# Experts' blocks: rows turned in float32 by TensorE instead of by transposing DMA copies

## The chip, the cores and the metric

The kernel runs on one core of one Trainium2 chip. The metric is the device time in microseconds (us) of the whole program, one launch. The core has five engines that run side by side: PE (TensorE, matmuls and their weight loads), DVE (VectorE), ACT (ScalarE), POOL (GpSimd) and SP (SyncE, which here only issues transfers). Each works through its own instructions in order; semaphores make one wait for another.

## The reference

Three layers follow one another on 1792 tokens (4 batches of 448) with 768 columns:

```
scores = 30 * tanh(q k^T / 8 / 30);  attn = exp(scores - max) / sum;  x = attn v        # 4 batches, 12 heads of 64
logits = x @ w_gate + modality_bias[modality_id];  e = argmax(logits);  g = softmax(logits)[e]
x[mask_e] = g * (relu(x[mask_e] @ w1[e]) @ w2[e])                                        # 8 experts, 768 -> 1024 -> 768
out = (sigmoid(x @ w_gate2) * (x @ w_val)) @ w_out                                       # 768 -> 1536 -> 768
```

The experts' products are taken in float16 parts: each float32 operand is a first part (rounded to float16) and a second part (what is left, in float16). Three of the four products of parts are added up, so each float32 product costs three float16 ones.

## The kernel before

**Attention** (0 to 296 us of the trace) goes through 24 pairs of heads in 96 slots of key tiles (`qk`, `exps`, `av`). The work that follows a batch (sums, gate logits, routing, token rows) is put into slots of the next batch by the table `AFTER`. `end2` makes 128 columns of a batch's token rows: TensorE turns four tiles of `OT` (L441), DVE multiplies by the reciprocal sums into the float32 tile `x` (L446), DVE makes the first part (L457) and POOL the second (L461), both into `xr`, which `x_write` and, for the last batch, `x_put` store to the table `xs` in DRAM.

**Experts.** The tokens are sorted into blocks of 128 of one expert each; with these inputs there are 15 blocks, numbered s = 0 to 14. For a block, SP loads its token list (`load_idx`), POOL adds up its two parts and gathers the rows from `xs` into one of two buffers `xg` (`gather`), SP's transposing DMA turns the rows into `xT` (`trx`, L740), PE multiplies by `w1s` (`mm1`, 36 matmuls), ACT and DVE take relu and its two parts from PSUM (`relu`, L761 and L762), SP's transposing DMA turns them into `hT` (`trh`, L765), PE multiplies by `w2s` (`mm2`, 48 matmuls), ACT and DVE scale (`put_y`, L784 and L785) and POOL scatters the rows to `ys`.

`step(s)` writes this out by hand: first product of block s, second product of block s - 1, transposes for s and s + 2, gather for s + 4. Beside it, blocks 4 to 10 each carry a set of float64 weights of the last layer: two loads (L865), DVE's three bit operations on each (L878, L879, L880), an ACT scale, and a store (L904). From block 5 on SP also turns finished rows of `ys` by DMA (`y_load`, L971). Where a block's expert is new (here blocks 4 and 12), 3 MB of `w1` and 3 MB of `w2` are loaded and split by ACT and DVE (L714, L718) inside an `If`.

All instructions of an engine keep the written order (`tc.manual_schedule()`), and so do SP's transfers: one that waits holds up those behind it. `tr_tile` hands out the PSUM banks in `M["trs"]` in turn, four of them during the experts.

**Last layer** (641 us to the end): seven-product multiplications of quarters (L1042, L1022) with operands made by ACT, DVE and POOL.

Of the kernel before, what the change touches and what calls it, by code (L numbers as in the profile page):

```python
# [8 lines left out]
F32 = mybir.dt.float32  # L9
# [51 lines left out]
# slots, after the last one of a batch's pairs, of the work that follows it; the third batch's goes ahead of the experts  # L61
AFTER = ({'g0': 0, 'g1': 2, 's': 3, 'e1s': 4, 'e1g': 5, 'route': 6, 'route_b': 8, 'ga': 9, 'gb': 10, 'gc': 12, 'sc': (10, 12, 14, 16), 'e2': (7, 10, 12, 17, 21, 24), 'lo': (1, 1, 1, 1, 1, 1), 'xw': (26, 27)}, {'g0': 1, 'g1': 2, 's': 3, 'e1s': 4, 'e1g': 5, 'route': 6, 'route_b': 10, 'ga': 9, 'gb': 10, 'gc': 12, 'sc': (10, 12, 14, 16), 'e2': (7, 10, 12, 17, 20, 23), 'lo': (1, 1, 1, 1, 1, 0), 'xw': (26, 27)}, {'g0': 1, 'g1': 2, 's': 3, 'e1s': 5, 'e1g': 5, 'route': 6, 'route_b': 7, 'ga': 10, 'gb': 11, 'gc': 13, 'sc': (10, 11, 12, 13), 'e2': (6, 9, 10, 11, 12, 13), 'lo': (1, 1, 2, 1, 1, 1), 'xw': (15, 15), 'ta': (9, 9), 'w1': (11, 11, 14, 12, 13, 13), 'w1s': (14, 15, 17, 17, 18, 19), 'idx': 16, 'gather': (18, 19, 23), 'trx': (20, 22), 'w2': (20, 21, 22, 22)})
# [3 lines left out]
def tile_kernel(ctx: ExitStack, tc: tile.TileContext, q, k, v, cap, mod, wg, mb, w1, w2, gw, vw, ow, out, dbg=None):  # L66
# [305 lines left out]
    def end0g(b, pp):  # L372
        """the gate's products with the sums over the values"""
# [94 lines left out]
    def x_put(h):  # L468
        """half of the last batch's columns"""
        c = DM // 4  # L470
        for a in range(2):
            w = slice(2 * c * a + c * h, 2 * c * a + c * h + c + (XW - DM if a == h == 1 else 0))
            nc.sync.dma_start(out=xs[(B - 1) * S:N, w].rearrange("(p c) n -> p c n", c=4), in_=xr[B - 1][:, :, w])

# [19 lines left out]
    def route_b(b):  # L494
        """place of each token in its expert's list: tokens of the expert before it"""
# [263 lines left out]
    def relu():  # L759
        hi, lo = (M["h"][:, a].rearrange("p (n f) -> p n f", n=2) for a in range(2))  # L760
# [38 lines left out]
    def step(s, fill=((), ()), more=None):  # L799
        """first product of block s, second product of block s - 1"""  # L800
# [8 lines left out]
        trh(s)  # L809
# [14 lines left out]
        mm2(s - 1)  # L824
# [842 lines left out]
```

## Time and profile before

| | us |
|---|---|
| median of three runs | 1146.42 (1144.09 to 1157.45) |
| span of the profiled execution | 1146.1 |
| attention, to the first product of block 0 | about 296 |
| blocks, to the end of the last second product | about 345 |
| last layer | about 505 |

No time from outside is given for the profiled execution, so its span stands for its time. PE is busy 930.1 us (81%), DVE 757.9, POOL 534.2, ACT 466.5. The page's slices show the DMA engines nearly full from the 14th slice to the 22nd, most of the stage of the blocks, and far less after that. A line such as L777 in the page is a line of this kernel; a group's idle time names what ended it.

### The profile page before, as it was taken

The numbers are of one execution on the slowest core, as the hardware profiler recorded it, in microseconds if no ns is written. First come the engines' busy times: TensorE is split into PE (matmuls) and PEld (weight loads), VectorE is DVE, ScalarE is ACT, GpSimd is POOL, SyncE is SP. The second block draws the span as 40 slices with busy tenths as digits, with TensorE's granted clock in tenths as the row PEclk, the third lists the DMA queues.
The fourth block names the chain that finished last, engine by engine and source line by source line (L and its number), as shares of the span: only waits on it lengthen the run. The fifth ranks groups of instructions, "written<-read, shape, count | busy, mean of one in ns | idle before, by whom it ended". The sixth has DMA issues, their size and how long they took to land. (4 is left out here: it accounts for less than half of the span.)

```text
span 1146.1 us, 14196 instructions
## 1 busy us (share of the span) xinstructions
PE 930.1 (81%) x4752; PEld 449.5 (39%) x4752; DVE 757.9 (66%) x1059; ACT 466.5 (41%) x734; POOL 534.2 (47%) x515
## 2 busy tenths in 40 slices
PE   7878677776877867795956788778898889999996
PEld 2223222222343433352523433333355545666653
DVE  7899989899662443435542389988657874543661
ACT  6656555555311332102331255445334434554330
POOL 5545536545432312214233577876603437877031
PEclk9898888887998989799979898999999999999998
DMA  9888976877756999999888333322304213220001
GB/s 200 173 192 142 169 174 109 163 154 183 203 130 143 206 210 184 244 194 260 144 201 117 114 122 123 113 97 83 110 15 96 84 55 97 84 70 28 1 28 55
DMA packets 202123, 150.98 MB, mean 132 GB/s; under 512 B 142240, under 2 KB 183088, under 8 KB 202032
## 3 DMA queue, kind: packets, MB, share of 16 engines
q1 hardware_dynamic: 196864, 130.37, 52.2%
q0 software_dynamic: 5168, 19.54, 6.5%
q8 instruction: 40, 0.66, 0.2%
q14 instruction: 51, 0.42, 0.1%
HBM read 87.05 MB, written 26.94 MB: 99 GB/s over the span
## 5 line engine op out<-in xcount | busy, mean ns | idle before, releaser
L777 PE MATMUL sc<-w2s,hs 128*128 128x384 f16 x720 | 133.6, 351 | 68.7 <-DMA hs<-hs 32.7
L1042 PEld LDWEIGHTS <-wa 128*128 128x128 f16 x909 | 90.5, 100 | 114.7 <-issue 39.3
L756 PE MATMUL sc<-w1s,xT 128*128 128x512 f16 x540 | 124.1, 390 | 12.2 <-DMA xT<-xg 12.2
L1042 PE MATMUL pp<-yr,wa 128*128 128x512 f16 (+1 forms) x468 | 107.8, 385 | 28.9 <-DVE zr L1072 12.9
L777 PEld LDWEIGHTS <-hs 128*128 128x128 f16 x720 | 74.5, 104 | 128.3 <-issue 45.6
L325 ACT ACTIVATE E<-sc,sct 128x896 f32<-128x896 f32 x72 | 72.4, 1005 | 95.2 <-PE sc L316 94.7
L940 POOL TENSOR_TENSOR wa<-sta,wa 128x384 f16<-128x384 f32 x87 | 92.1, 1073 | 6.5 <-ACT wa L935 6.4
L913 DVE TENSOR_TENSOR sta<-sta 128x384 f32<-128x384 f32 x96 | 89.6, 971 | 2.1 <-POOL y L940 0.7
L316 PE MATMUL sc<-qT,kT 128*128 128x448 f16 x288 | 77.2, 396 | 13.7 <-DMA qT<-qT 10.1
L756 PEld LDWEIGHTS <-xT 128*128 128x128 f16 x540 | 53.6, 100 | 79.1 <-DMA xT<-xg 13.7
L350 POOL TENSOR_TENSOR w2s<-E 128x896 f32<-128x896 f32 x24 | 51.5, 2146 | 63.5 <-ACT E L330 63.3
L1042 PE MATMUL pp<-zr,wa 128*128 128x384 f16 x441 | 75.7, 326 | 0.6 <-ACT yr L1090 0.6
L1042 PE MATMUL pp<-wos,yr 128*128 128x384 f16 x378 | 67.3, 343 | 10.3 <-ACT hs L1135 10.3
L330 ACT ACTIVATE E<-E,capt 128x896 f32<-128x896 f32 x72 | 74.7, 1038 | 0.6
L339 PE MATMUL ot<-E,vf 128*64 128x448 f32 x288 | 72.5, 586 | 0.0
L725 POOL TENSOR_TENSOR idx<-idx 128x1 f32<-128x1 f32 x19 | 6.9, 363 | 119.5 <-DMA idx<-lists 119.3
L935 ACT ACTIVATE wa<-sta 128x384 f16<-128x384 f32 x98 | 48.5, 513 | 23.5 <-DVE sta L913 19.7
L352 POOL TENSOR_TENSOR w2s<-w2s,E 128x896 f32<-128x896 f32 x24 | 52.0, 2165 | 9.7 <-ACT E L330 8.6
L316 PEld LDWEIGHTS <-kT 128*128 128x128 f16 x288 | 25.3, 104 | 77.9 <-issue 48.9
L1042 PEld LDWEIGHTS <-wb 128*128 128x128 f16 x378 | 37.6, 100 | 44.3 <-issue 11.6
L1042 PEld LDWEIGHTS <-yr 128*128 128x128 f16 x378 | 38.6, 102 | 39.0 <-issue 16.6
L358 DVE TENSOR_TENSOR w2s<-w2s,EM 64x448 f32<-64x448 f32 x48 | 51.4, 1071 | 2.0 <-POOL w2s L352 1.5
(308 smaller groups left out, 1741.1 us busy)
## 6 DMA issues: line engine op xcount, KB each, us to landing
sta<-g SPq DMA_DIRECT2D x40, 384.0 KB, 3.0
st<-in_moe_w_dram SPq DMA_DIRECT2D x8, 1536.0 KB, 14.0
sta<-in_moe_w_val_dram SPq DMA_DIRECT2D x12, 768.0 KB, 7.9
sta<-in_moe_w_out_dram SPq DMA_DIRECT2D x12, 768.0 KB, 4.2
g<-sta SPq DMA_DIRECT2D x18, 384.0 KB, 5.8
qf<-in_q_dram SPq DMA_DIRECT2D x24, 224.0 KB, 4.0
qT<-qT SPq DMA_DIRECT2D x46, 112.0 KB, 3.1
kf<-in_k_dram SPq DMA_DIRECT2D x24, 192.0 KB, 3.3
```

What stands on the lines that cost most here:

```text
L316: nc.tensor.matmul(sc[:, h, :S], kt_[:, 3 * h + j], qt_[:, w, h], start=w == 0, stop=w == 1)
L325: nc.scalar.activation(out=e, in_=src, func=AF.Tanh, scale=sct)
L330: nc.scalar.activation(out=e, in_=e, func=AF.Exp, scale=capt)
L339: nc.tensor.matmul(ot[g][64 * h:64 * h + 64, :S], vf[g][:, h, j], e[:, h], start=j == 0, stop=False)
L350: nc.gpsimd.tensor_tensor(out=Tt[g], in0=Et[n - 1], in1=Et[n], op=ALU.add)
L352: nc.gpsimd.tensor_tensor(out=Tt[g], in0=Tt[g], in1=Et[n], op=ALU.add)
L358: nc.vector.tensor_tensor(out=Tt[g][p, h], in0=Tt[g][p, h], in1=e[p], op=ALU.add)
L756: nc.tensor.matmul(p[:, nh], xT[s % 2][:, a, kk], w1s[:, b_, kk, 512 * nh:512 * nh + 512], start=i == 0, stop=i == 17)
L777: nc.tensor.matmul(M["p2"][:, nh, :384], hT[par][:, a, kk], w2s[:, b_, kk, 384 * nh:384 * nh + 384], start=i == 0, stop=i == 23)
L913: tt = lambda eng, o, x, y, op: eng.tensor_tensor(out=o, in0=x, in1=y, op=op)
L940: los = [lambda x=x, d=d, e=e: e.tensor_tensor(out=d[1], in0=x, in1=d[0], op=ALU.subtract) for x, d, e in todo]
L1042: nc.tensor.matmul(bk[c][:, c0:c1], l(p, a, kk), r(p, b_, kk)[:, c0:c1], start=i == c0 == 0 and p in (1, 2, 7), stop=i == 3 * kn - 1 and c ...
```

## The change

`end2` writes float32 rows straight into `xr`; the split into two parts goes, with its temporary tiles and the entries `lo` of `AFTER`. So `xs` and the gathered rows hold float32 (the same bytes a row). A new helper `turned` lets PE turn float32 columns into two PSUM banks in turn; ACT copies each to the first parts, DVE takes the difference for the second parts. `trx` and `trh` call it in place of the transposing DMAs. `relu` becomes one ACT instruction that writes float32. In `step`, `trh(s)` stands between the two halves of `mm2(s - 1)`, and before the loop likewise. The other differences are removed comments and the views that go with these edits.

```
@@ end2
-        if spread:
-            xx = M["x32"][i]
-        else:
-            xx = tail.tile([112, 4, 2, D], F32, name="x32", tag="x32", bufs=2)
         nc.vector.tensor_tensor(
-            out=xx,
+            out=xr[b][:, :, 128 * i:128 * i + 128].rearrange("p c (a d) -> p c a d", a=2),
...
-        if spread:
-            nc.scalar.activation(out=hi, in_=src, func=AF.Copy)
-            end2_lo(b, i, nc.gpsimd if i in (0, 1, 3, 4, 5) else nc.vector)
-        else:
-            nc.vector.tensor_copy(hi, src)
-
-    def end2_lo(b, i, eng=nc.gpsimd):
-        src, hi, lo = x32.pop((b, i))
-        eng.tensor_tensor(out=lo, in0=src, in1=hi, op=ALU.subtract)
@@ x_put: two transfers of 1.5 KB a row in place of four of half that
+        w = slice(DM // 2 * h, (DM // 2, XW)[h])
+        nc.sync.dma_start(out=xs[(B - 1) * S:N, w].rearrange("(p c) n -> p c n", c=4), in_=xr[B - 1][:, :, w])
@@ transposes
+    def turned(dst, src, n):
+        for q_ in range(2):
+            pt = tr_tile()
+            for c in range(n):
+                w = 128 * (n * q_ + c)
+                nc.tensor.transpose(pt[:, 128 * c:128 * c + 128], src[:, w:w + 128], id32)
+            hi, lo = (dst[:, a, n * q_:n * q_ + n].rearrange("p k n -> p (k n)") for a in range(2))
+            nc.scalar.activation(out=hi, in_=pt[:, :128 * n], func=AF.Copy)
+            nc.vector.tensor_tensor(out=lo, in0=pt[:, :128 * n], in1=hi, op=ALU.subtract)
     def trx(s):
         nc.gpsimd.tensor_copy(gt[s % 4], xg[s % 2][:, DM:DM + 1])
-        nc.sync.dma_start_transpose(out=xT[s % 2].rearrange("p a k n -> p (a k) n"), in_=xg[s % 2].bitcast(F16)[:, 0:2 * DM])
+        turned(xT[s % 2], xg[s % 2], 3)
@@ relu, trh
-        nc.scalar.activation(out=hi, in_=M["p1"], func=AF.Relu)
-        nc.vector.scalar_tensor_tensor(out=lo, in0=M["p1"], scalar=0.0, in1=hi, op0=ALU.max, op1=ALU.subtract)
+        nc.scalar.activation(out=M["h"].rearrange("p (n f) -> p n f", n=2), in_=M["p1"], func=AF.Relu)
     def trh(s):
-        nc.sync.dma_start_transpose(out=hT[s % 2].rearrange("p a k n -> p (a k) n"), in_=M["h"].rearrange("p a f -> p (a f)"))
+        turned(hT[s % 2], M["h"], 4)
@@ step (and the same before the loop)
-        trh(s)
...
-        mm2(s - 1)
+        mm2(s - 1, (0,))
+        trh(s)
+        mm2(s - 1, (1,))
```

Where instructions stand now, at the two places on which the prediction turns. First PE just ahead of `mm1(2)`: the end of `mm2(0)` (input `hs`, weights `w2s`), then what follows. Before:

```order
L777 LDWEIGHTS hs
L777 MATMUL sc<-w2s,hs 128x384
L756 LDWEIGHTS xT_116
L756 MATMUL sc<-w1s,xT_116 128x512
L756 LDWEIGHTS xT_116
```

Now:

```order
L766 LDWEIGHTS hs
L766 MATMUL sc<-w2s,hs 128x384
L1349 UNCONDITIONAL_BRANCH
L1354 UNCONDITIONAL_BRANCH
L832 UNCONDITIONAL_BRANCH
L724 MATMUL tr<-id_85,xg_115 128x128 x6
L747 LDWEIGHTS xT_116
L747 MATMUL sc<-w1s,xT_116 128x512
```

The six transposes of `trx(3)` stand ahead of `mm1(2)`; before, they were a transfer on SP and PE went straight on.

Second DVE in `step(4)`, the first that carries float64 weights (`sta`): before, from the second part of relu to `put_y`:

```order
L762 SCALAR_TENSOR_TENSOR hs<-sc,hs 128x1024
L686 TENSOR_LOAD tib
L833 COMPARE_AND_BRANCH
L718 SCALAR_TENSOR_TENSOR w1s<-st_111,w1s 128x1024 x6
L833 UNCONDITIONAL_BRANCH x2
L878 TENSOR_SCALAR sta<-sta 128x768
L879 SCALAR_TENSOR_TENSOR sta<-sta 128x768
L880 SCALAR_TENSOR_TENSOR sta<-sta 128x768
```

Now:

```order
L727 TENSOR_TENSOR xT_116<-tr,xT_116 128x384 x2
L868 TENSOR_SCALAR sta<-sta 128x768
L869 SCALAR_TENSOR_TENSOR sta<-sta 128x768
L870 SCALAR_TENSOR_TENSOR sta<-sta 128x768
L868 TENSOR_SCALAR sta<-sta 128x768
L869 SCALAR_TENSOR_TENSOR sta<-sta 128x768
L870 SCALAR_TENSOR_TENSOR sta<-sta 128x768
L727 TENSOR_TENSOR hs<-tr,hs 128x512 x2
L774 SCALAR_TENSOR_TENSOR y<-sc,gt_131,y 128x768
```

The second parts of h (`hs<-tr`, the operand of `mm2(4)`) stood ahead of the float64 operations and stand behind them now.

## Rows read from the trace of the kernel before

**Rows 1.** Windows by stage: PE, PEld, DVE, ACT, POOL busy, PEclk, DMA, GB/s.

```profile
0.00:296.00 296.00, 219.10 (x1005) 75.82 (x1005) 268.50 (x395) 169.25 (x199) 159.85 (x130) 0.88 0.79 165
...
390.00:641.00 251.00, 190.25 (x974) 98.49 (x972) 105.82 (x131) 59.58 (x75) 73.14 (x102) 0.89 0.99 195
641.00:935.00 294.00, 248.85 (x1193) 120.21 (x1192) 236.04 (x277) 130.50 (x257) 167.15 (x138) 0.94 0.29 90
```

**Rows 2.** Timeline of PE, blocks 3 to 14: start, us, work, idle before.

```profile
382.82 9.41 PE L756 MATMUL sc<-w1s,xT 128*128 128x512 f16 x36 [4.70 <-DMA xT<-xg]
...
399.87 7.93 PE L756 MATMUL sc<-w1s,xT 128*128 128x512 f16 x36
419.06 10.07 PE L777 MATMUL sc<-w2s,hs 128*128 128x384 f16 x48 [11.26 <-DMA hs<-hs]
...
591.96 10.65 PE L777 MATMUL sc<-w2s,hs 128*128 128x384 f16 x48 [13.14 <-DMA hs<-hs]
...
611.88 7.96 PE L777 MATMUL sc<-w2s,hs 128*128 128x384 f16 x48 [1.49 <-ACTq L802]
621.92 3.11 PE L1042 MATMUL pp<-yr,wa 128*128 128x256 f16 x27 [2.08 <-DMA perm<-idx,dix]
631.79 9.52 PE L777 MATMUL sc<-w2s,hs 128*128 128x384 f16 x48 [6.76 <-ACTq L1447]
```

**Rows 3.** Timeline of SP (transfers issued), blocks 4 to 14 and their ends.

```profile
394.57 17.26 SPq L765 DMA_TRANSPOSE hs<-hs  x1
...
413.03 5.20 SPq L740 DMA_TRANSPOSE xT<-xg  x1
...
614.67 2.04 SPq L765 DMA_TRANSPOSE hs<-hs  x1
618.53 1.69 SPq L740 DMA_TRANSPOSE xT<-xg  x1
```

**Rows 4.** DMA issues of the whole program: count, us from issue to landing.

```profile
yr<-ys SPq DMA_TRANSPOSE x8, 5.9
```

**Rows 5.** Timeline of PE around block 2.

```profile
319.69 1.47 PE L441 MATMUL tr<-id,OT 128*112 128x128 f32 x12
321.00 7.96 PE L777 MATMUL sc<-w2s,hs 128*128 128x384 f16 x48
328.80 7.93 PE L756 MATMUL sc<-w1s,xT 128*128 128x512 f16 x36
```

**Rows 6.** Timeline of SP in the same stretch.

```profile
333.54 3.46 SPq L473 DMA_DIRECT2D xs<-xr  x4
337.09 5.58 SPq L765 DMA_TRANSPOSE hs<-hs  x1
343.55 3.97 SPq L722 DMA_DIRECT2D idx<-lists  x4
351.58 1.53 SPq L740 DMA_TRANSPOSE xT<-xg  x1
```

**Rows 7.** Timeline of POOL and DVE in the same stretch.

```profile
347.70 1.00 POOL L734 DMA_INDIRECT xg<-xs,idx  x1 [0.67 <-POOL idx L727]
...
360.54 1.01 POOL L734 DMA_INDIRECT xg<-xs,idx  x1 [0.28 <-POOL idx L727]
...
333.58 0.09 DVE L546 MEMSET xr<- 112x32 f32 x1 [3.98 <-POOL xr L461]
```

**Rows 8.** Groups by line: count, busy us, mean ns of one, idle before.

```profile
L457 DVE CAST xr<-x 112x512 f16<-112x512 f32 x18 | 14.1, 783 | 0.6
...
L1072 DVE TENSOR_TENSOR hs<-hs,pp 128x512 f32<-128x512 f32 x18 | 12.2, 679 | 5.2 <-PE pp L1042 3.8 <-ACT sta L935 1.4
L1090 ACT ACTIVATE hs<-pp 128x512 f32<-128x512 f32 x18 | 10.4, 580 | 4.3 <-PE pp L1042 4.3
```

**Rows 9.** Groups by line, DVE alone, from 345 to 641 us.

```profile
L879 DVE SCALAR_TENSOR_TENSOR sta<-sta 128x768 int32<-128x768 int32 x14 | 13.4, 960 | 0.5
...
L878 DVE TENSOR_SCALAR sta<-sta 128x768 int32<-128x768 int32 x14 | 7.8, 559 | 51.8 <-DMA sta<-in_moe_w_val_dram 32.6 <-DMA sta<-in_moe_w_gate_dram 19.0
```

More of the change, by code (lines that the diff above doesn't have):

```diff
@@ L60 @@
 ZBT = (0, 0, 0, 1, 1, 2, 3, 5, 6)
-AFTER = ({'g0': 0, 'g1': 2, 's': 3, 'e1s': 4, 'e1g': 5, 'route': 6, 'route_b': 8, 'ga': 9, 'gb': 10, 'gc': 12, 'sc': (10, 12, 14, 16), 'e2': (7, 10, 12, 17, 21, 24), 'lo': (1, 1, 1, 1, 1, 1), 'xw': (26, 27)}, {'g0': 1, 'g1': 2, 's': 3, 'e1s': 4, 'e1g': 5, 'route': 6, 'route_b': 10, 'ga': 9, 'gb': 10, 'gc': 12, 'sc': (10, 12, 14, 16), 'e2': (7, 10, 12, 17, 20, 23), 'lo': (1, 1, 1, 1, 1, 0), 'xw': (26, 27)}, {'g0': 1, 'g1': 2, 's': 3, 'e1s': 5, 'e1g': 5, 'route': 6, 'route_b': 7, 'ga': 10, 'gb': 11, 'gc': 13, 'sc': (10, 11, 12, 13), 'e2': (6, 9, 10, 11, 12, 13), 'lo': (1, 1, 2, 1, 1, 1), 'xw': (15, 15), 'ta': (9, 9), 'w1': (11, 11, 14, 12, 13, 13), 'w1s': (14, 15, 17, 17, 18, 19), 'idx': 16, 'gather': (18, 19, 23), 'trx': (20, 22), 'w2': (20, 21, 22, 22)})
+AFTER = ({'g0': 0, 'g1': 2, 's': 3, 'e1s': 4, 'e1g': 5, 'route': 6, 'route_b': 8, 'ga': 9, 'gb': 10, 'gc': 12, 'sc': (10, 12, 14, 16), 'e2': (7, 10, 12, 17, 21, 24), 'xw': (26, 27)}, {'g0': 1, 'g1': 2, 's': 3, 'e1s': 4, 'e1g': 5, 'route': 6, 'route_b': 10, 'ga': 9, 'gb': 10, 'gc': 12, 'sc': (10, 12, 14, 16), 'e2': (7, 10, 12, 17, 20, 23), 'xw': (26, 27)}, {'g0': 1, 'g1': 2, 's': 3, 'e1s': 5, 'e1g': 5, 'route': 6, 'route_b': 7, 'ga': 10, 'gb': 11, 'gc': 13, 'sc': (10, 11, 12, 13), 'e2': (6, 9, 10, 11, 12, 13), 'xw': (15, 15), 'ta': (9, 9), 'w1': (11, 11, 14, 12, 13, 13), 'w1s': (14, 15, 17, 17, 18, 19), 'idx': 16, 'gather': (18, 19, 23), 'trx': (20, 22), 'w2': (20, 21, 22, 22)})
 @with_exitstack
@@ L433, in rows, with end2 @@
         return xr[b]
-    x32 = {}
-    def end2(b, i, spread=False):
+    def end2(b, i):
         rows(b)
@@ L441, in end2 @@
             nc.tensor.transpose(xp[:112, 128 * c:128 * c + 128], OT[NPAIR * b + i][:, 112 * c:112 * c + 112], id32)
-        if spread:
-            xx = M["x32"][i]
-        else:
-            xx = tail.tile([112, 4, 2, D], F32, name="x32", tag="x32", bufs=2)
         nc.vector.tensor_tensor(
-            out=xx,
+            out=xr[b][:, :, 128 * i:128 * i + 128].rearrange("p c (a d) -> p c a d", a=2),
             in0=xp[:112].rearrange("p (c a d) -> p c a d", c=4, a=2),
             in1=recs[b][:, :, 2 * i:2 * i + 2].rearrange("p c (a o) -> p c a o", o=1).to_broadcast([112, 4, 2, D]), op=ALU.mult)
-        hi, lo = (xr[b].bitcast(F16)[:, :, DM * a + 128 * i:DM * a + 128 * i + 128] for a in range(2))
-        src = xx.rearrange("p c a d -> p c (a d)")
-        x32[b, i] = src, hi, lo
-        if spread:
-            nc.scalar.activation(out=hi, in_=src, func=AF.Copy)
-            end2_lo(b, i, nc.gpsimd if i in (0, 1, 3, 4, 5) else nc.vector)
-        else:
-            nc.vector.tensor_copy(hi, src)
-    def end2_lo(b, i, eng=nc.gpsimd):
-        src, hi, lo = x32.pop((b, i))
-        eng.tensor_tensor(out=lo, in0=src, in1=hi, op=ALU.subtract)
     def x_write(b, h):
@@ L468, in x_put @@
     def x_put(h):
[L470 to L473, printed above, removed]
+        w = slice(DM // 2 * h, (DM // 2, XW)[h])
+        nc.sync.dma_start(out=xs[(B - 1) * S:N, w].rearrange("(p c) n -> p c n", c=4), in_=xr[B - 1][:, :, w])
     def route(b):
@@ L759, in relu @@
     def relu():
-        hi, lo = (M["h"][:, a].rearrange("p (n f) -> p n f", n=2) for a in range(2))
-        nc.scalar.activation(out=hi, in_=M["p1"], func=AF.Relu)
-        nc.vector.scalar_tensor_tensor(out=lo, in0=M["p1"], scalar=0.0, in1=hi, op0=ALU.max, op1=ALU.subtract)
+        nc.scalar.activation(out=M["h"].rearrange("p (n f) -> p n f", n=2), in_=M["p1"], func=AF.Relu)
     def trh(s):
-        nc.sync.dma_start_transpose(out=hT[s % 2].rearrange("p a k n -> p (a k) n"), in_=M["h"].rearrange("p a f -> p (a f)"))
+        turned(hT[s % 2], M["h"], 4)
     def mm2(s, halves=(0, 1)):
@@ L1226, in tile_kernel @@
                 add(n0 + o["e2"][i], end2, b, i)
-                add(n0 + o["e2"][i] + o["lo"][i], end2_lo, b, i)
             for i in range(2):
@@ L1319, in tile_kernel @@
         hs = mid.tile([128, 6 * F], F16, name="hs")
-        M["h"] = hs[:, 0:2 * F].rearrange("p (a f) -> p a f", a=2)
+        M["h"] = hs[:, 0:2 * F].bitcast(F32)
         hT = [hs[:, 2 * F * i:2 * F * (i + 1)].rearrange("p (a k n) -> p a k n", a=2, k=8) for i in (1, 2)]
@@ L1324, in tile_kernel @@
         M["glast"] = mid.tile([128, 1], F32, name="glast")
-        M["x32"] = [yr[:112, 1024 * i:1024 * i + 1024].bitcast(F32).rearrange("p (c a d) -> p c a d", c=4, a=2) for i in range(12, 18)]
         st0 = yr[:, 0:12 * F].bitcast(F32).rearrange("p (k f) -> p k f", f=F)
@@ L1343, in tile_kernel @@
             scatter(B - 1, c)
-        end2(B - 1, 0, True)
-        end2(B - 1, 1, True)
+        end2(B - 1, 0)
+        end2(B - 1, 1)
         for c in range(2, 4):
             scatter(B - 1, c)
-        end2(B - 1, 2, True)
+        end2(B - 1, 2)
         split_w(st1, w2s, hi=None, parts=(5,))
         mm1(1, (1,))
-        end2(B - 1, 3, True)
-        end2(B - 1, 4, True)
-        end2(B - 1, 5, True)
+        end2(B - 1, 3)
+        end2(B - 1, 4)
+        end2(B - 1, 5)
         relu()
@@ L1359, in tile_kernel @@
         x_put(1)
-        trh(1)
         load_idx(3)
@@ L1363, in tile_kernel @@
             load_w(1, 1, st1, v2)
-        mm2(0)
+        mm2(0, (0,))
+        trh(1)
+        mm2(0, (1,))
         with if_new(1, [ENG.Activation, ENG.DVE]):
```

## The prediction

> **What bounds the kernel now.** I read the windows by stage first. In attention DVE is busy 268.5 of 296 us, in the stage of the blocks no engine is: PE has 190.25 of 251 us, DVE 105.82, but the DMA share is 0.99 at 195 GB/s [rows 1]. After 641 us the same engines move 90 GB/s at a share of 0.29, which is 90 / 0.29 = 310 GB/s when full [rows 1]. So the bytes of the blocks cost more DMA time than bytes elsewhere. Then PE's timeline: a block needs 7.93 us for its first product and 7.96 us for its second where PE was not waiting before [rows 2, 5], 15.9 us together, but from the start of `mm1(4)` at 382.82 to the end of `mm2(13)` at 611.88 + 7.96 = 619.84 us eleven steps take 237.0 us, 21.5 each [rows 2]. PE waits, and the longest waits are for transposes of h by DMA: 11.26 and 13.14 us, and the product that follows is itself longer, 10.07 and 10.65 us [rows 2]; I call such a first product after a wait cold. Last SP: a transpose held SP's queue for 17.26 us, others for 5.20 and 5.58 [rows 3, 6], and loads of lists and weights stand behind it. The blocks are bounded by the DMA engines and by SP's order, not by PE.
>
> **DMA time removed.** From 390 to 641 us eleven transposes of h go out (first at 394.57, last at 614.67) and eleven of x (first at 413.03, last at 618.53) [rows 3]. They carry 11 x (0.52 + 0.39) = 10.1 MB of 251 us x 195 GB/s = 48.9 MB; the eight `y_load` transposes [rows 4], which stay, carry 3.1. The other 35.7 MB at 310 GB/s take 115 us, so the transposes take 0.99 x 251 - 115 = 133 us. In tiles of 128 x 128 that is 11 x 28 + 8 x 12 = 404, so 0.33 us a tile (an estimate) and 9.2 us of all DMA engines a block. What stays is 251 - 101 = 150 us, under 14 us a block: DMA stops being the limit.
>
> The Trainium skill speaks against this: "Advanced Engine Details and Errata", section X-Bar Transpose (TRN2), says that transpose DMAs are as fast as regular ones. By that rule only 10.1 of 48.9 MB goes, 52 us of 251, and the DMA would still want 17.1 us a block; the rows above disagree with it, since the same engines reach 310 GB/s at full share elsewhere. It is the first rival below.
>
> **PE work added.** Fourteen float32 transposes a block, six for x and eight for h. Twelve of `OT` take 1.47 us end to end, the next matmul starting at 321.00, 1.31 after [rows 5]: 0.11 to 0.125 us each. I take 0.125, since these have 128 columns where those have 112: 1.75 us a block, all on PE's path. So PE's floor is 15.9 + 1.75 = 17.65 us a step, 194 us for eleven.
>
> **ACT and DVE work.** ACT gets four copies a block, by the nearest row 0.58 us for 512 columns and less for 384 [rows 8]: 2.2 us. DVE gets four differences at up to 0.68 [rows 8], some 2.5 us, and loses relu's second part. With that ACT is some 40% busy in a stage of 214 us, DVE 56%. For h there is cover: the transposes follow 4 us of `mm2(s - 1)`, and the copies have the other 4 us and `mm1(s + 1)`. What this costs if the cover goes is the third rival.
>
> **Steps 4 to 14.** Floor 194 us, plus 1 us a step that I leave for loads of new experts, late scatters and the cold starts after them: 205 against 237, **-32 us**. Bounds: -43 at the floor; on the other side only the waits named after the DMA transposes go, 11.26 + 13.14 + 4.70 = 29, and the new transposes cost 11 x 1.75 = 19, so -10. I lean to the floor, because two waits that name ACT or DVE end in the same transfers, and PE already had products back to back where nothing waited.
>
> **Last block.** From 619.84 us to the end of `mm2(14)` at 631.79 + 9.52 = 641.3 it takes 21.5 us, of which 3.11 is the next layer's first piece and 9.52 a cold product [rows 2]. With scatters landing sooner I take 15.5, **-6** (bounds 0 and -10).
>
> **Bridge from block 2 to block 4.** Here the change adds a wait. `mm1(2)` ran from 328.80 while the gather for block 3 was on its way; now `trx(3)` stands ahead of it on PE. That gather was issued at 347.70 [rows 7], SP's transpose of its rows went out at 351.58 [rows 6]. It will come sooner: `x_put` waited 3.98 us for POOL's split [rows 7], and the list loads stood behind a 5.58 us transpose [rows 6]. Both go, so about 8 us: rows in at 343, `mm1(2)` cold until 353. The next gather, at 360.54 [rows 7] about 9 us earlier, lands at 356, so `trx(4)` waits 2 us; `mm2(1)`, `mm1(3)` and `mm2(2)` with their transposes follow and `mm1(4)` starts near 384 against 382.82: **+1** (bounds -10, if the rows come 10 us sooner than I think, and +14, if nothing comes sooner: the 15 us by which `mm1(2)` slips).
>
> **Attention.** 18 casts go, 14.1 us of DVE [rows 8], and POOL's 18 subtractions; DVE gets about 2.2 us for blocks 0 and 1. DVE is 91% busy, but its wait for PE and transfers takes part of the gain, and a cast's mean hides POOL's interference, which the next operation may meet. I take half, **-6** (bounds -14 and +2).
>
> **Last layer.** Nothing there changes: 0, with 4 either way for what the clock and the pieces prepared in the blocks do.
>
> **Sum.** -32 - 6 + 1 - 6 = -43: 1146.1 - 43 = **1103 us**. The span of 1146.1 is 0.3 below the median of the runs, so no correction.
>
> **Rivals.**
> - *DMA still sets the pace.* If a transposed byte costs what any byte costs, a step wants 21.5 x (1 - 10.1 / 48.9) = 17.1 us of DMA and 17.65 of PE, and half of today's 21.5 - 15.9 = 5.6 us of waiting a step would stay: 20.5 a step, -12 there, -3 at the last block: 1146.1 - 12 - 3 + 1 - 6 = 1126. For: the share is at 0.99. Against: 310 GB/s [rows 1], and SP's 17 us transposes. 14%.
> - *PE waits for gathers in order.* Each `trx(s + 2)` now stops PE if the rows are late. If every step loses 4 us so, 1103 + 44 = 1147, no change. Against: a gather is issued at the end of a step and needed 8 us into the second step after, over 20 us later; only blocks 3 and 4 lack that. 6%.
> - *DVE holds h back: slower.* The second parts of h now stand behind six float64 operations whose loads DVE waited for 51.8 us in seven steps, 7.4 each [rows 9]. PE needs h 18.4 us after `mm1(s)` ends (1.75 of transposes, `mm2(s - 1)`, `mm1(s + 1)`, 0.75 more). DVE's own work there is 2.5 us of differences and, for two units, one operation of 0.56 and two of 0.96 us each [rows 9], 5 us, so a load may be 10 us late. From there each us costs one in seven steps; if all of today's 51.8 came on top, 1103 + 52 = 1155. For: the order. Against: the loads then have the DMA engines to themselves and SP is not held up ahead of them. 4%.
> - *More comes.* Attention gives 14, the bridge 8, the blocks reach the floor and the last block 10: 1103 - 8 - 9 - 11 - 4 = 1071. 14%.
> - *Clock.* If float32 transposes let the clock drop, products take 10.07 and 9.41 [rows 2] in place of 7.96 and 7.93, 3.6 us a step, 1103 + 40 = 1143. Against: the second product right after twelve transposes took 7.96 [rows 5]. 2%.
>
> The forecast keeps 60%, with its own range of 1086 to 1120. The **range** of 1078 to 1128 leaves out most of the big gain and the cases near 1145, some 2 in 10. Two per cent, about what a measurement can tell here, is 1123 and 1169. Faster by more: 0.60 + 0.14 + 0.05 of the DMA case = 0.79 and some of the tails, 0.81; slower by more needs two mishaps together, 0.03; within, 0.16.
>
> **What would show it.** In the trace after, the DMA share of the blocks falls to about 0.7 and GB/s stay near 200; steps come every 18 to 19 us; `mm2` no longer waits for DMA; transposes take 0.125 us; PE stands idle for 12 to 15 us ahead of the transposes for block 3. Wrong would be: a share still near 1 (first rival); PE waiting for `xg` at later blocks (second); `mm2` waiting for DVE's second parts of h behind the float64 operations (third). If attention ends at 296 us as before, that term was wrong; if at 282, it was all DVE.

## The result and the profile after

The changed kernel took 1114.74 us (median of 4 runs, 1111.19 to 1120.62), the kernel before 1150.24 in runs on the same chip: a ratio of 0.968 with a 95% interval of 0.961 to 0.976. The profiled execution took 1114.88 us, with a span of 1113.1. Divided at the same five events, and against the profiled execution of before, the time went here (us):

| part | before | after | difference | forecast |
|---|---|---|---|---|
| start to `mm2(0)` | 321.0 | 310.1 | -10.9 | -6 |
| `mm2(0)` to `mm1(4)` (the bridge) | 61.8 | 74.4 | +12.5 | +1 |
| `mm1(4)` to the end of `mm2(13)`, steps 4 to 14 | 237.0 | 210.3 | -26.7 | -32 |
| to the end of `mm2(14)`, last block | 21.5 | 19.8 | -1.6 | -6 |
| last layer | 504.8 | 498.5 | -6.3 | 0 |
| span | 1146.1 | 1113.1 | -33.0 | -43 |

The forecast of the bridge was the place of `mm1(4)`, 384 us, and that is where it started (384.45). But the attention ended 10.9 us earlier and all of it was lost on the way there: by that product the forecast had -5, the trace has +1.6.

The windows by stage of the changed kernel (PE, PEld, DVE, ACT, POOL busy with counts, PEclk, DMA share, GB/s), which answer to [rows 1]:

```profile
0.00:286.00 286.00, 216.23 (x1017) 76.13 (x1018) 241.16 (x380) 172.03 (x205) 141.10 (x118) 0.90 0.86 181
390.00:595.00 205.00, 187.84 (x1054) 106.86 (x1051) 117.92 (x162) 78.81 (x119) 63.56 (x91) 0.97 0.82 176
615.00:912.00 297.00, 255.12 (x1242) 124.77 (x1241) 241.47 (x286) 132.94 (x263) 170.24 (x141) 0.95 0.29 91
```

In the blocks PE is busy 92% of the stretch, where it was 76%; the DMA share went from 0.99 to 0.82. PE's timeline around the bridge and the first steps, and at two later waits (start, us, work, idle before), answers to [rows 2, 5]:

```profile
310.09 4.06 PE L766 MATMUL sc<-w2s,hs 128*128 128x384 f16 x24
313.99 1.04 PE L724 MATMUL tr<-id,hs 128*128 128x128 f32 x8
314.86 4.06 PE L766 MATMUL sc<-w2s,hs 128*128 128x384 f16 x24
335.62 1.51 PE L724 MATMUL tr<-id,xg 128*128 128x128 f32 x6 [16.69 <-DMA xg<-xs,idx]
336.92 9.48 PE L747 MATMUL sc<-w1s,xT 128*128 128x512 f16 x36
355.58 1.51 PE L724 MATMUL tr<-id,xg 128*128 128x128 f32 x6 [9.18 <-DMA xg<-xs,idx]
356.89 5.86 PE L766 MATMUL sc<-w2s,hs 128*128 128x384 f16 x24
...
375.12 0.82 PE L724 MATMUL tr<-id,xg 128*128 128x128 f32 x6
375.78 4.06 PE L766 MATMUL sc<-w2s,hs 128*128 128x384 f16 x24
379.68 1.04 PE L724 MATMUL tr<-id,hs 128*128 128x128 f32 x8
380.55 4.06 PE L766 MATMUL sc<-w2s,hs 128*128 128x384 f16 x24
384.45 7.93 PE L747 MATMUL sc<-w1s,xT 128*128 128x512 f16 x36
...
401.55 7.93 PE L747 MATMUL sc<-w1s,xT 128*128 128x512 f16 x36
...
451.44 1.51 PE L724 MATMUL tr<-id,xg 128*128 128x128 f32 x6 [6.21 <-DMA xg<-xs,idx]
...
531.34 1.51 PE L724 MATMUL tr<-id,xg 128*128 128x128 f32 x6 [8.84 <-DMA xg<-xs,idx]
```

Three things stand here. The two long waits of the bridge are for gathered rows, ahead of the transposes of blocks 3 and 4. Where nothing waits, a step is 17.10 us (384.45 to 401.55), its fourteen transposes take 0.66 + 0.87 = 1.53 us from start to start, and the second products behind them need 4.06 us a half, the pace of before. Later waits are all for gathered rows too; the waits of PE from 390 to 600 us (total, times, longest) are one line:

```profile
PE tr L724 <- DMA xg<-xs,idx: 16.8, 4, 8.8
```

The waits for DMA transposes of h of [rows 2] are gone. POOL in the bridge answers to [rows 7]:

```profile
322.31 0.93 POOL L498 DMA_INDIRECT lists<-pf,pi  x1 [7.37 <-DMA lists<-pf,pi]
329.92 0.19 POOL L705 TENSOR_TENSOR idx<-idx 128x1 f32<-128x1 f32 x1 [6.68 <-DMA idx<-lists]
...
331.27 1.00 POOL L714 DMA_INDIRECT xg<-xs,idx  x1 [0.64 <-POOL idx L707]
...
341.30 0.98 POOL L782 DMA_INDIRECT perm<-idx,dixa  x1 [7.73 <-DMA perm<-idx,dixa]
...
344.96 1.01 POOL L714 DMA_INDIRECT xg<-xs,idx  x1 [0.55 <-POOL idx L707]
```

The gather for block 3 goes out at 331.27, 16.4 us sooner than in [rows 7], the one for block 4 at 344.96, 15.6 sooner. A scatter to the lists waits for the one before, the list load for the last of them, the gather for the load; and the gather for block 4 stands behind a scatter that waited 7.73 us. Its rows reached PE 10.6 us after its issue.

### The profile page after: what moved, and what is told of

Read it like the earlier page. It is cut to its first block, busy times and chain, and to the rows that moved or that the text cites. A ratio compares the mean times of both kernels' runs of the same rounds, so it can differ in the third digit from the quotient of the medians.

```text
span 1113.1 us, 14641 instructions
## 1 busy us (share of the span) xinstructions
PE 938.6 (84%) x4974; PEld 472.7 (42%) x4974; DVE 751.2 (67%) x1089; ACT 492.0 (44%) x792; POOL 507.9 (46%) x492
## 5 line engine op out<-in xcount | busy, mean ns | idle before, releaser
L766 PE MATMUL sc<-w2s,hs 128*128 128x384 f16 x720 | 126.5, 334 | 0.1
L747 PE MATMUL sc<-w1s,xT 128*128 128x512 f16 x540 | 120.9, 382 | 0.0
L350 POOL TENSOR_TENSOR w2s<-E 128x896 f32<-128x896 f32 x24 | 53.7, 2237 | 100.8 <-ACT E L330 100.8
L903 DVE TENSOR_TENSOR sta<-sta 128x384 f32<-128x384 f32 x96 | 92.0, 996 | 3.8 <-POOL y L930 2.4
L316 PE MATMUL sc<-qT,kT 128*128 128x448 f16 x288 | 75.3, 387 | 21.2 <-DMA qT<-qT 10.6
L766 PEld LDWEIGHTS <-hs 128*128 128x128 f16 x720 | 72.2, 100 | 46.4 <-issue 4.9
L727 DVE TENSOR_TENSOR xT<-tr,xT 128x384 f16<-128x384 f32 x34 | 17.8, 554 | 87.6 <-ACT xT L726 79.6
L724 PE MATMUL tr<-id,xg 128*128 128x128 f32 x102 | 18.0, 320 | 48.8 <-DMA xg<-xs,idx 46.5
L925 ACT ACTIVATE wa<-sta 128x384 f16<-128x384 f32 x98 | 48.4, 513 | 13.6 <-DVE sta L903 11.7
L1032 PEld LDWEIGHTS <-yr 128*128 128x128 f16 x378 | 38.5, 102 | 37.5 <-issue 15.1
```

The source lines that it names most:

```text
L316: nc.tensor.matmul(sc[:, h, :S], kt_[:, 3 * h + j], qt_[:, w, h], start=w == 0, stop=w == 1)
L350: nc.gpsimd.tensor_tensor(out=Tt[g], in0=Et[n - 1], in1=Et[n], op=ALU.add)
L747: nc.tensor.matmul(p[:, nh], xT[s % 2][:, a, kk], w1s[:, b_, kk, 512 * nh:512 * nh + 512], start=i == 0, stop=i == 17)
L766: nc.tensor.matmul(M["p2"][:, nh, :384], hT[par][:, a, kk], w2s[:, b_, kk, 384 * nh:384 * nh + 384], start=i == 0, stop=i == 23)
L903: tt = lambda eng, o, x, y, op: eng.tensor_tensor(out=o, in0=x, in1=y, op=op)
L1032: nc.tensor.matmul(bk[c][:, c0:c1], l(p, a, kk), r(p, b_, kk)[:, c0:c1], start=i == c0 == 0 and p in (1, 2, 7), stop=i == 3 * kn - 1 and c ...
```

## The experiments

Each part is divided as above, from one profiled execution a kernel, which can lie some us from the median of its runs (e1's took 1106.1 us, e8's 1078.3); the medians are of 4 runs, the ratio is to runs of the kernel before on the same chip (0.968 for the changed kernel). Nine profiles, that of the changed kernel and those of e2 to e5 and e8 to e11, have the same attention: `mm2(0)` starts between 307.3 and 316.8 us in them (mean 311.4), so a few us there say nothing.

| kernel | `mm2(0)` at | bridge | steps 4-14 | last block | last layer | median | ratio (95%) |
|---|---|---|---|---|---|---|---|
| e1_h_by_pe | 322.2 | 59.2 | 207.9 | 17.0 | 498.1 | 1116.7 | 0.976 (0.970-0.983) |
| e2_x_by_pe | 307.3 | 73.4 | 212.7 | 22.4 | 499.1 | 1121.6 | 0.981 (0.974-0.989) |
| e3_block3_rows | 316.8 | 77.8 | 209.3 | 20.7 | 498.0 | 1126.4 | 0.974 (0.967-0.982) |
| e4_bridge_order | 310.3 | 58.6 | 208.3 | 21.1 | 499.0 | 1094.0 | 0.954 (0.948-0.960) |
| e5_lists_first | 312.0 | 71.3 | 201.4 | 18.9 | 498.6 | 1103.6 | 0.962 (0.956-0.968) |
| e8_both_orders | 307.4 | 58.1 | 194.2 | 18.3 | 498.5 | 1086.7 | 0.949 (0.943-0.955) |
| e9_scatter_first | 312.4 | 56.1 | 196.7 | 18.4 | 498.4 | 1087.7 | 0.950 (0.944-0.956) |
| e10_transpose_added | 312.3 | 71.5 | 214.8 | 18.5 | 498.8 | 1117.6 | 0.973 (0.965-0.980) |
| e11_copy_added | 313.9 | 71.8 | 208.3 | 18.9 | 498.8 | 1110.2 | 0.966 (0.960-0.971) |
| e7_casts_back | 311.3 | 73.9 | 212.4 | 20.8 | 499.6 | 1118.4 | 0.966 (0.958-0.973) |
| e12_subtractions_back | 324.0 | 73.9 | 210.5 | 20.5 | 500.9 | 1129.7 | 0.976 (0.968-0.985) |
| e13_both_back | 331.1 | 72.7 | 207.5 | 19.2 | 497.8 | 1134.2 | 0.980 (0.973-0.987) |

### One half at a time

e1 is the kernel before with `turned` for h alone, and `mm2` in two halves around it; e2 is the changed kernel with the old `relu` and `trh`, and `mm2` in one piece:

```diff
 e1, against before
-        hi, lo = (M["h"][:, a].rearrange("p (n f) -> p n f", n=2) for a in range(2))
-        nc.scalar.activation(out=hi, in_=M["p1"], func=AF.Relu)
-        nc.vector.scalar_tensor_tensor(out=lo, in0=M["p1"], scalar=0.0, in1=hi, op0=ALU.max, op1=ALU.subtract)
+        nc.scalar.activation(out=M["h"].rearrange("p (n f) -> p n f", n=2), in_=M["p1"], func=AF.Relu)
...
-        nc.sync.dma_start_transpose(out=hT[s % 2].rearrange("p a k n -> p (a k) n"), in_=M["h"].rearrange("p a f -> p (a f)"))
+        turned(hT[s % 2], M["h"], 4)
```

> Only h goes by TensorE; x keeps its two float16 parts made in the attention and its transposing DMA copies. Theory (each part brings its own gain; a tile of 128x128 costs all DMA engines 0.33 us): the attention ends as before (mm2(0) starts near 321 us, not 310); no product waits for x on PE, so mm1(4) starts near 378, 57 after mm2(0); a step wants 21.5 - 16 x 0.33 = 16.2 us of DMA, less than PE's 17, so steps 4 to 14 take some 213 us, with waits of mm1 for transposed x where the rows come late; DMA share there near 0.88. Total near 1118. Rival (transposed bytes cost what other bytes cost): the DMA engines keep the pace, steps 4 to 14 take 228 us and the total is near 1135. Rival 2 (x's transposes alone caused the late gathers): steps as in the full change, 210, since mm1 waits for the same rows.

> Only x goes by TensorE; h keeps its float16 parts and transposing DMA copies. Theory: the attention's gain stays whole (mm2(0) near 310 us), the bridge to block 4 is as long as in the full change or longer (75 to 80 us from mm2(0) to mm1(4)), mm2's waits for DMA of h come back at several steps, 10 us and more each; steps 4 to 14 take 222 to 232 us. Total near 1130. Rival (the transposes of x were the ones that filled the DMA queue and h's then are quick): steps 4 to 14 at 212, total near 1116.

Either half takes nearly all of the steps' gain: 207.9 and 212.7 us against 210.3 with both and 237.0 without. So the gains do not add: a step takes 18.9 and 19.3 us, and 19.1 with both, where PE's own work is 16.4, 16.2 and 17.1 (estimates from the products and transposes above). In the changed kernel the rest is late rows: with the list loads moved, its steps fall to 201.4 and 194.2 (e5 and e8 below). The halves were not run with that order, so what is shown is that the second half gained nothing while the lists came late. The DMA share, which I took as the sign, does not tell the halves from the kernel before; the windows of e1 and then e2 over 390 to 585 us:

```profile
390.00:585.00 195.00, 175.53 (x947) 95.34 (x946) 98.79 (x129) 65.82 (x91) 64.63 (x86) 0.96 1.02 203
```

```profile
390.00:585.00 195.00, 170.14 (x893) 90.59 (x892) 112.87 (x139) 63.24 (x89) 60.21 (x75) 0.94 1.00 201
```

A share at 1 stays in both, where I had expected 0.88 for e1, with PE as busy as 90% and 87%. The total of e1 is that of its theory (1118), that of e2 lies between theory and rival. In the steps e2's theory missed: its second products waited 4.2 us in all for DMA transposes of h, not 10 and more at several steps, and 212.7 us is the rival's number (212). The attention's gain belongs to x alone (322.2 with h alone), and so does the longer bridge (59.2 with h alone): what x's half brings in the one it gives back in the other, and the whole change is hardly faster than h's half.

### The price of a transposing copy

In steps 4 to 9, into columns that nothing reads, against the changed kernel:

```diff
+            if 3 < s < 10:
+                src = hT[(s - 1) % 2].rearrange("p a k n -> p (a k n)")
+                nc.sync.dma_start_transpose(out=M["spare"], in_=src)              # e10
+                nc.sync.dma_start(out=M["spare"].rearrange("p k n -> p (k n)"), in_=src)  # e11 in its place
```

> The full change with one more transposing DMA copy in each of steps 4 to 9: 16 tiles of 128x128 float16 (0.52 MB), from the parts of h of the block before into columns that nothing reads; no result changes. Theory (0.33 us of all DMA engines a tile): 5.3 us each, 32 us in all, so the DMA busy time from 390 us to the end of block 9 rises by some 30 us (share to about 1) and the total by 5 to 20, to 1120 to 1135. Rival (a transposed byte costs what any byte costs): 1.7 to 2.6 us each, 10 to 16 us of DMA time in all, as in e11_copy_added, total within 5 of the changed kernel.

> The same as e10_transpose_added with a plain copy of the same 0.52 MB in place of each transposing one. Theory and rival agree here: 1.7 to 2.6 us of all DMA engines each at the 200 to 310 GB/s of the block stage, 10 to 16 us in all; total within 5 of the changed kernel's 1114. What counts is the difference to e10_transpose_added in DMA busy time: some 18 us by the theory, 0 by the rival.

The hardware DMA queue over the whole program (packets, MB, share of 16 engines) in the changed kernel, in e10 and in e11:

```profile
q1 hardware_dynamic: 138080, 115.82, 45.5%
```

```profile
q1 hardware_dynamic: 150560, 118.96, 48.6%
```

```profile
q1 hardware_dynamic: 138944, 118.96, 46.2%
```

Of the spans of 1113.1, 1115.8 and 1111.6 us that is 506.5, 542.3 and 513.6 us (a tenth of a per cent is 1.1 us): 35.8 us for six transposing copies, 7.1 for six plain ones of the same bytes, 6.0 against 1.2 us each. By tile of 128x128 the transposing copy costs 0.37 us; the prediction's estimate was 0.33. The Trainium skill's "Advanced Engine Details and Errata", section X-Bar Transpose (TRN2), says that the two are as fast as each other; these rows disagree, about five to one. SP's timeline shows a second cost, the time for which the copy held the queue: 44.7 us over the six in e10 (first and last shown), 2.7 in e11.

```profile
389.70 16.05 SPq L802 DMA_TRANSPOSE yr<-hs  x1
...
491.01 8.48 SPq L802 DMA_TRANSPOSE yr<-hs  x1
```

```profile
391.62 0.19 SPq L802 DMA_DIRECT2D yr<-hs  x1
...
486.85 0.50 SPq L802 DMA_DIRECT2D yr<-hs  x1
```

The price was as the theory had it, the effect on the whole was not: 7.5 us between the medians of e10 and e11, and e10 not measurably slower than the changed kernel. 36 us of DMA time mostly fitted in the share that was free.

### The bridge and the gathers

e3 moves the transposes of block 3's rows, with the gather for block 5, behind `mm1(2)`; e4 moves those of block 4 and 5 as well:

```diff
 e4, against the changed kernel; trx(3) and gather(5) leave the prelude
-            trx(s + 2)
+            if s > 3:
+                trx(s + 2)
...
+        if s == 2:
+            trx(3)
+            gather(5)
+        if s == 3:
+            trx(4)
+            fetch(6)
+            trx(5)
         put_y(gt[(s - 1) % 4], rows_of(s - 1))
         put_perm(s)
-        if s < NFULL:
+        if 2 < s < NFULL:
             fetch(s + 4)
```

> The full change with one group moved: the transposes of block 3's rows on PE, and with them the gather for block 5 on POOL, stand behind mm1(2) and the load of block 4's weights, ahead of those of block 4's rows, not ahead of mm1(2). Theory (PE's order is the cost): mm1(2) fills the first wait of 16.7 us, but the transposes of block 4's rows still stand ahead of mm2(1) and wait for rows that land at 355, so mm1(4) starts at 376 to 380 in place of 384.5 and the total is 4 to 8 below the changed kernel. Rival (the chain of lists and gathers sets the end): mm1(4) at 382 to 385, total within 2 of the changed kernel.

> The full change, with the transposes of x rows of blocks 3, 4 and 5 on PE behind mm1(2), mm2(1) and so on: trx(3) with the gather for block 5 at the end of step 2, trx(4), the fetch for block 6 and trx(5) at the end of step 3; from step 4 on nothing moves. Theory A (the slip of mm1(2) behind late rows is the bridge's cost; PE's order decides): the wait of 16.7 us before trx(3) is filled with mm1(2) and mm2(1); mm1(4) starts near 366 us in place of 384.5 and the total falls by 15 to 20, to 1095 to 1100. Theory B (the chain of transfers up to the rows of block 4, which land at 355.5 whatever PE does, and the gathers after it set the end): mm1(4) comes to 376 to 384 or the steps behind it wait longer for gathers, and the total falls by 0 to 6, to 1109 to 1114.

e3 missed: moving the first batch alone shortened nothing, 77.8 us. In its timeline `mm1(2)` runs at once, but the transposes of block 4's rows still stand ahead of `mm2(1)` and wait longer, 22.81 us:

```profile
325.46 7.93 PE L747 MATMUL sc<-w1s,xT 128*128 128x512 f16 x36
341.60 1.51 PE L724 MATMUL tr<-id,xg 128*128 128x128 f32 x6 [8.21 <-DMA xg<-xs,idx]
365.92 1.51 PE L724 MATMUL tr<-id,xg 128*128 128x128 f32 x6 [22.81 <-DMA xg<-xs,idx]
```

With both batches moved (e4) three products run in that time and the bridge falls to 58.6 us, less than before the change. The wait that is left has another name:

```profile
318.92 7.93 PE L747 MATMUL sc<-w1s,xT 128*128 128x512 f16 x36
326.69 4.06 PE L766 MATMUL sc<-w2s,hs 128*128 128x384 f16 x24
...
337.03 7.73 PE L747 MATMUL sc<-w1s,xT 128*128 128x512 f16 x35 [0.20 <-DVE xT L727]
356.69 6.27 PE L766 MATMUL sc<-w2s,hs 128*128 128x384 f16 x24 [11.93 <-ACT hs L751]
```

So PE's order was the cost, theory A: 1094.0 us, and an interval that lies below that of the changed kernel. POOL's order, which the edit touches too, was not: the gathers for blocks 4 and 5 go out at 344.71 and 347.11 us in e4, at 344.96 and 347.25 in the changed kernel. The later steps did not change (208.3); their waits are the next experiment. In the changed kernel POOL waits for list loads in nearly every step; SP issues one at 426.19, right behind a bulk load, and POOL has it at 441.06. The two engines' timelines:

```profile
423.76 1.16 SPq L855 DMA_DIRECT2D sta<-in_moe_w_val_dram  x2
426.19 0.92 SPq L702 DMA_DIRECT2D idx<-lists  x2
```

```profile
441.06 0.19 POOL L705 TENSOR_TENSOR idx<-idx 128x1 f32<-128x1 f32 x1 [12.76 <-DMA idx<-lists]
```

e5 issues the list loads first:

```diff
+        if s < NFULL:
+            load_idx(s + 4)
         for f in fill[0]:
             f()
...
-            fetch(s + 4)
+            gather(s + 4)
```

> The full change, with the three list loads of a block's gather (0.5 KB each) issued on SP ahead of the bulk float64 loads and stores and of the loads that wait for scatters, not behind them; the gather itself stays at the end of the step. Theory (POOL gets the lists some 12 us late because they stand behind bulk transfers in SP's queue, and that makes PE's 16.8 us of waits for x rows in steps 4 to 14): those waits shrink to under 3 us and steps 4 to 14 take 192 to 197 us in place of 210; total 1098 to 1102. Rival (the gather of 128 rows lands late itself, or the lists wait for something else): POOL's wait for lists falls, the waits of PE for rows stay over 10 us, total 1110 to 1114.

The theory held in kind: POOL's waits for list loads, 63.2 us in six steps of the changed kernel, are gone, and PE's waits for rows from 365 to 600 us fell from 16.8 to 4.3 us. In size it missed: the steps fell to 201.4 us, where it had 192 to 197, and some of the waiting went to ACT:

```profile
PE tr L724 <- DMA xg<-xs,idx: 4.3, 1, 4.3
PE sc L766 <- ACTq L791: 3.3, 1, 3.3
PE sc L766 <- ACTq L825: 1.9, 1, 1.9
```

> The bridge's order of e4_bridge_order together with the early list loads of e5_lists_first (for blocks 8 and up). Theory (the two costs lie in different stretches and add): mm1(4) starts near 369 us, steps 4 to 14 take some 200 us, and the total is that of the changed kernel less 20 and less 10, 1080 to 1086. Rival (the earlier bridge only brings the later gathers closer to PE, so that what one gives the other takes): steps 4 to 14 at 208 or more as in e4_bridge_order, total 1092 to 1096.

> As e8_both_orders, and the scatter of block 0's results goes out on POOL ahead of the gather for block 3 and of both scatters of the row numbers, the second of which moves behind the gather for block 5. In e4_bridge_order PE waited 11.93 us before mm2(2) for relu of block 3, which stood on ACT behind the eviction of block 1, and that behind the landing of block 0's scatter (issued 342.4, landed 354). Theory: that wait goes to 3 us or less, mm1(4) starts near 360, total 8 to 10 below e8_both_orders. Rival (the rows of block 4 come as late as before, since POOL's queue and the transfers set them): mm1(4) at 366 to 369, total as e8_both_orders.

e8, which is e4 and e5 together, adds the two: 58.1 and 194.2 us in its profile, the fastest of its four runs, and a median of 1086.7, just above the theory's 1080 to 1086; the ratio is 0.949 (0.943 to 0.955), clear of the changed kernel's interval. In its steps no wait of PE for rows is left. e9, whose edit against e8 is

```diff
+        put_y(gt[0], rows_of(0))
         gather(3)
         put_perm(0)
-        put_perm(1)
         load_idx(4)
-        put_y(gt[0], rows_of(0))
...
             gather(5)
+            put_perm(1)
```

took the wait before `mm2(2)` away, as expected, and gained nothing: `mm1(4)` starts at 368.49. PE's wait has only moved behind ACT's split of block 4's weights, which stands ahead of the copies of h on ACT and waits for the weights (PE first, then ACT):

```profile
347.02 4.06 PE L766 MATMUL sc<-w2s,hs 128*128 128x384 f16 x24
...
367.16 1.54 PE L724 MATMUL tr<-id,xg 128*128 128x128 f32 x6 [10.65 <-DVE hs L727]
```

```profile
361.92 2.95 ACT L694 ACTIVATE w1s<-st 128x1024 f16<-128x1024 f32 x3 [7.48 <-DMA st<-in_moe_w_dram]
364.77 1.06 ACT L726 ACTIVATE hs<-tr 128x512 f16<-128x512 f32 x2
```

The rival was right that it would bring nothing, but not on why: not the rows but the load of the weights is next.

### The attention

```diff
 e7 (in end2, against the changed kernel)
+        if b < B - 1:
+            spare = tail.tile([112, 4, 128], F16, name="spare")
+            nc.vector.tensor_copy(spare, xr[b][:, :, 128 * i:128 * i + 128])
 e12, in place of the last line
+            nc.gpsimd.tensor_tensor(out=spare, in0=xr[b][:, :, 128 * i:128 * i + 128], in1=M["zz"], op=ALU.subtract)
```

e12's `zz` is a tile of zeros. e13 has the cast, and POOL's subtraction of its result behind it.

> The full change with the 18 DVE casts of x rows of the first three batches put back (112x512 float32 to float16, into columns that nothing reads); POOL's 18 subtractions stay out, and no result changes. Theory (DVE's time sets the attention's end, and the casts alone made the 10.9 us): mm2(0) starts at 318 to 322 us in place of 310, and the total is 8 to 12 above the changed kernel, 1122 to 1127. Rival (half of the gain came from POOL's subtractions, which held up DVE and the rows' ways out): mm2(0) at 313 to 316, total 3 to 6 above.

> The full change with POOL's 18 subtractions (112x512, float32 less float16) put back into the first three batches of the attention, on rows already made and into columns that nothing reads; the DVE casts stay out, and no result changes. Since the casts alone gave back 1.2 us of 10.9. Theory (POOL's subtractions were the cost: 24.9 us of POOL, beside which DVE's operations took longer, 1071 ns against 885 for 64x448): mm2(0) starts at 315 to 320 us in place of 310, DVE's 64x448 mean is back at 1020 ns or more, total 4 to 10 above the changed kernel. Rival (neither; x's transposing DMA copies and the parts' path at the attention's end made it): mm2(0) at 309 to 312, total within 3.

> The full change with both put back as they were, the DVE cast first and POOL's subtraction of its result from the row behind it, 18 of each. Theory (the two together made the attention's 10.9 us): mm2(0) at 318 to 323 us, total 8 to 12 above the changed kernel. Rival (what is left of the 10.9 us lies in the transposing DMA copies of x at the attention's end): mm2(0) at 311 to 316.

e7's theory, which was the prediction's main reason, fell: with 15.1 us of casts back on DVE, `mm2(0)` starts at 311.3, within the spread of kernels without them. POOL's subtractions alone move it to 324.0, outside the range of the nine, and the total to 0.976, an interval that overlaps the changed kernel's; both to 331.1, more than the 321.0 of before, which stays open. The kernel before had most subtractions one or two slots behind the cast (`lo` in `AFTER`), these two have them at once, so neither is quite its order. Groups of the first 300 us, of the changed kernel and then of e12 (count, busy, mean):

```profile
L358 DVE TENSOR_TENSOR w2s<-w2s,EM 64x448 f32<-64x448 f32 x48 | 45.2, 942 | 0.6
L250 DVE TENSOR_SCALAR qs<-qf 112x512 f16<-112x512 f32 x23 | 19.0, 826 | 1.5 <-DMA qf<-in_q_dram 1.4
```

```profile
L358 DVE TENSOR_TENSOR w2s<-w2s,EM 64x448 f32<-64x448 f32 x46 | 46.5, 1011 | 0.5
L250 DVE TENSOR_SCALAR qs<-qf 112x512 f16<-112x512 f32 x23 | 25.7, 1116 | 1.2 <-DMA qf<-in_q_dram 1.1
L449 POOL TENSOR_TENSOR spare<-xr,zz 112x512 f16<-112x512 f32 x18 | 24.2, 1342 | 37.2 <-DVE xr L443 37.0
```

One cost can be read, a second is possible. DVE's own operations are longer beside POOL's: its four largest groups of the first 300 us (L358, L250, L251 and L245 by 384 columns) add up to 133.6, 133.6, 129.4 and 127.1 us in the kernel before, e1, e12 and e13, which have the subtractions, and to 112.7 to 121.3 in the ten profiles that do not (e12 and e13 have two and four operations of L358 still to come). Single groups go either way (from the changed kernel to e12: L250 826 to 1116 ns, L358 942 to 1011, L251 1409 to 1433, L245 1028 to 1008). Over 0 to 286 us DVE is busy 249.7 us against 241.2, with nothing added to it. The Trainium skill's "Trainium Architecture — The Big Picture", section What this means for kernel authors, says that DVE and GpSimd share a port pair under an exclusive lock; the longer operations agree with a shared port, and no run here shows that it is a lock. The possible second cost: POOL, in order, stood 37.0 us for rows from DVE, with the sums of the exponentials queued behind. But its wait for ACT ahead of those sums (L350) fell from 100.8 to 60.6 us at the same time, so it is not shown that this cost anything. How the 13 us divide between the two was not separated.

## Why the prediction came out as it did

**The total.** The median is 11.7 us above the forecast of 1103 and inside the range; the ratio gives 0.968 x 1146.4 = 1110. The mechanism held (transposes by PE cost little, those by DMA cost much), and four terms of the sum were mis-sized: the forecast was too good by 6.6 us up to the start of `mm1(4)`, by 5.3 in steps 4 to 14 and by 4.4 in the last block, and too bad by 6.3 in the last layer. That last one was luck: nothing in the argument foresaw it, and it cancelled 6.3 of the 16.3 us by which the others missed.

**DMA time removed.** Where transposing copies were added, a tile cost 0.37 us, near the 0.33 of the prediction, and the first rival's rule fell with it. The transposes that the change took out gave back less. SP's queue in the kernel before, over the whole program:

```profile
q1 hardware_dynamic: 196864, 130.37, 52.2%
```

That is 598.3 us against 506.5 after: 92 us for the 444 tiles that went (h of 15 blocks, x of 17), 0.21 us each, where 0.33 would have made 147. The weak step was to put all other bytes of the blocks at 310 GB/s. After the change the share there is 0.82 at 176 GB/s, which is 215 GB/s when full, and not the forecast's 0.7 near 200. Why a tile costs more when added than it gives back when removed stays open.

The step from a share of 0.99 to "DMA is the limit" was also weaker than I wrote: e1 and e2 run at a share of 1 with 24 to 29 us gained. The DMA engines may still set the pace in these two: each half took 51 us off the queue (49.6% of 1104.3 and 49.1% of 1114.9 us are left), 3.4 a block, and 21.5 less 3.4 is 18.1 us a step (an estimate), near the 18.9 and 19.3 measured. SP's queue, held 2.7 to 16.1 us by one added copy, fits as well. No experiment separates these two, since every transposing copy has both costs.

**Steps 4 to 14.** Floor and allowance both missed, in opposite directions. The floor was 188 us (11 x 17.10), not 194: the transposes take 0.109 us each, not 0.125, and the products 15.57 a step from start to start, where I had added two durations that overlap at their ends. Against that, the 11 us left for late loads were 22.2: 16.8 of waits for rows and the cold starts after them. This is the second rival in part (PE waits for gathers in order), to which I had given 6 in 100 because a gather is issued 20 us ahead. I had counted from the end of a step, not from the list load in front of the gather, which came 12.76 us late behind bulk loads; e5 shows that this was the cause of most of it (16.8 to 4.3 us).

**Bridge and attention.** The rows of block 4 came where I put them (forecast 356, traced 355.6), those of block 3 7 us sooner (343 and 335.6), and `mm1(4)` started at its place. But those places were times of the trace before, less what I took off for earlier gathers, with no gain of the attention in them. The mistake was to book that gain beside them as if the bridge would move with it. PE's order, with rows ahead of products that need none of them, turned the earlier end into waiting; e4 gives it back by order alone. For the attention itself the size was too small and the reason mostly wrong: not the 14.1 us of DVE casts that I halved, but, by one profile each of e7 and e12, POOL's subtractions, which I had named without a price.

**DVE holding h back** (third rival) did not come: DVE's wait for the float64 loads, 51.8 us in [rows 9], fell to 17.3, and no second product waits for it. Its group from 345 to 610 us:

```profile
L868 DVE TENSOR_SCALAR sta<-sta 128x768 int32<-128x768 int32 x14 | 7.8, 554 | 17.3 <-DMA sta<-in_moe_w_val_dram 16.7 <-DMA sta<-in_moe_w_gate_dram 0.5
```

**The clock** did not fall either: granted 0.97 in the blocks against 0.89, with the float32 transposes in the stream.

**Last block and last layer.** Of the 6 us at the last block 1.6 came: a wait of 6.49 us for DVE's queue stands where 6.76 for ACT's was [rows 2]:

```profile
601.25 5.55 PE L1032 MATMUL pp<-yr,wa 128*128 128x256 f16 x27 [6.49 <-DVEq L1380]
```

The last layer is 6 us shorter in the changed kernel and 4 to 7 in all twelve experiments, whichever half they have. 3.54 us of it is one wait for POOL's queue at 647.38 us in the trace of before, which the changed kernel does not have; what made it, and the rest, was not tried.

## What to carry to other kernels

When a transfer is replaced by work on the engine that consumes it, that engine now waits in order for the transfer's source: put the new work behind everything that does not need it, and follow the chain of small loads in front of it back to their place in the queue. Where two costs lie on one resource, test the halves before adding their gains: here either half took nearly all, as long as the lists came late. And price what is taken off a neighbouring engine too; the 18 operations on POOL were worth more than those on the engine that looked busy.

## What the runs showed of the hardware

- A transposing DMA copy of 0.52 MB, added, took 6.0 us of all 16 engines, a plain one 1.2, and the queue's packets rose by 12,480 against 864 for six of them. The 444 tiles of transposes that the change removed gave back 0.21 us each.
- The same transposing copy held SP's queue for 2.7 to 16.1 us, a plain one for 0.2 to 0.5.
- Float32 transposes of 128x128 in a dense stream start every 0.109 us, and the product behind them runs at its full pace; the mean of one in the groups reads 0.273 us for those of h, since their records overlap.
- A load of 0.5 KB issued behind two of 768 KB on the same queue was seen by its reader about 15 us later (426.19 to 441.06); with such loads issued first, the reader's waits for them, 63.2 us in six steps, were gone.
- Beside POOL's 18 subtractions, the four largest groups of DVE in the attention took 127 to 134 us in place of 113 to 121.
